# The sums' bank read by the Newton steps, weight pieces formed in a PSUM bank, and a dense list that knows what is left

## The chip, the cores and the metric

The kernel runs on one core of a Trainium2 chip, in one launch. The metric is the time of an execution in microseconds (us) on the device. Before the change the median of three runs is 644.42 us (642.54 to 644.81). The engines are named as the profile names them: PE (TensorE, matmuls), PEld (its weight loads), DVE (VectorE), ACT (ScalarE), POOL (GpSimd) and SP (SyncE, which issues the DMAs).

## The reference

Three layers follow each other. The attention works on 2 batches of 8 heads, 1152 keys, a head width of 64, and queries pooled by twos to 576:

```
q_pool = q.reshape(B, H, S // 2, 2, D).mean(axis=3)
scores = scale * q_pool @ k^T;  scores -= max over the keys
attn = exp(scores);  attn = attn / (sum over the keys + 1e-09)
out = attn @ v                            # 2 x 8 x 576 x 64
x = out.transpose(0, 2, 1, 3).reshape(1152, 512)
h = x @ w_in                              # 512 -> 2048
x = (max(h, 0) + log1p(exp(-|h|))) @ w_out         # -> 512
h = max(x @ w1, x @ w2, x @ w3)           # 512 -> 768, three times
out = h @ w_out2                          # -> 512
```

The dense weights arrive as 64-bit numbers, which the kernel reads as pairs of 32-bit words and turns into float32 itself.

## The kernel before

**Numbers in two halves.** A matmul of full float32 precision is made of three of the type fp32r: a value is cut into a high half (a copy to fp32r) and a low half (value minus high half), and high x high, low x high and high x low are added up in PSUM (`matmul3`, L1341).

**Attention.** The 16 heads are taken as 8 pairs. Each pair is prepared (load, pool the queries, transpose, cut into halves, send copies by DMA), then a first pass (`scores`, `part_max`, L977 on DVE) finds the maximum of each query's scores, and then units follow: two for each pair, three for the first, 17 in all, most of 288 queries. A unit goes through nine blocks of 128 keys and both heads: scores transposed (`st`, L1044 and L1045), their exponential (`p`, L1052 on ACT), a running sum over the blocks (`acc`, L1061, on POOL; in the last unit on DVE), and the product with the values (`x`, L1069). At a unit's end `sum_up` (L1081) adds over the keys by a matmul with ones into a PSUM bank `l`. `keep_sum` (L1086, ACT) copies it to SBUF as `rr` with 1e-9 added, `log_sum` and `near_inverse` (L1093, L1097, ACT) form exp(-ln(rr)) in `rz`, two Newton steps (`inverse`, L1103 and L1105, DVE) form -1/sum in `rr` out of `rr` and `rz`, both in SBUF, and `divide` (L1117, DVE) multiplies `x` from PSUM by it.

**Weight pieces.** The dense weights are cut into 56 pieces of 128 x 512. A piece is loaded (`raw`, SP), then `size_weight` (L232, ACT) and `bound_weight` (L237, POOL) treat its upper words, three integer steps on DVE (`float_weight`, L248, L257, L261) put the float32 number together in a tile `t`, `high_weight` (L276, ACT) and `low_weight` (L281, DVE) cut it. The first nine (NPRE) are formed while the attention runs, in a tile `t` in SBUF; the others in the dense part, where `t` lies in a PSUM bank, `b0`.

**Banks.** In the attention two of the eight PSUM banks hold `x`; the other six are a ring `s`, from which each block of scores, each transpose and each sum takes one and gives it back.

**Dense part.** The 1152 rows are three chunks of 384. `up` (h = x @ w_in, twelve matmuls for a block of 128 columns) is followed by the softplus (`size_h`, `lost1`, `lost2`, `log_h`, `lost3`, `soft`: ACT, DVE and POOL by turns), its halves (`high_g` ACT, `low_g` DVE), and, four blocks later, `down` (y). Gates (m) and `final` (o) follow.

**What sets the order.** All of it is issued in an order that a list planner (`Order.ordered`) writes. Each work item has an engine, a cost in us, a place (its priority), what it reads and writes, and perhaps a bank that it takes or frees. The planner moves a clock for each engine, takes the work that can begin first, and among those ready on its engine the one with the lowest place. The attention and the first pieces are one list, the dense part with the later pieces is a second one, whose engine clocks begin at 0. Each engine then works through its own queue in that order, so that a late item holds up what is behind it. The constants in AK, WINDOW and the costs in `order.add` only set this order.

Of the kernel before, what the change touches and what calls it, by code (L numbers as in the profile page):

```python
# [16 lines left out]
P = 128  # L17
# [16 lines left out]
AK = {"load": 30.79, "load1": -203.6, "q1": -64.7, "k1": -43.43, "v0": -70.5, "s0": -51.42, "v": -50.88, "q": -48.24, "k": -39.97, "pass": 7.12, "gap": 2.74, "values": 6.34, "sum": 8.99, "p1": -78.35, "p2": -9.81, "kl": 0.75}  # L34
WINDOW = 31.77
POOL_OF = {"tq": "s", "tk": "s", "tm": "s", "sum": "s"}
# [18 lines left out]
class Order:  # L55
# [6 lines left out]
    def __init__(self, **pools):  # L62
        self.work = []
        self.wrote = {}
        self.read = {}
        self.pools = pools
        self.got = {}

# [15 lines left out]
    def ordered(self):  # L84
# [6 lines left out]
        clear = dict.fromkeys(self.AFTER, 0.0)  # L91
# [7 lines left out]
        for _ in work:  # L99
# [26 lines left out]
            for m in users[n]:  # L126
                left[m] -= 1
                if not left[m]:
                    other = work[m][0]
                    ready[other][m] = max(  # L130
                        at[k] + (self.AFTER[work[k][0]] if work[k][0] != other or other in ("SP", "AQ") else 0.0)
                        for k in work[m][5]
                    )
        return [n for _, n in out]
# [3 lines left out]
def kernel(  # L138
# [100 lines left out]
    def float_weight(n, step):  # L239
        r, size = words[n][:2]  # L240
        if step == 0:
            if n < NPRE:
                words[n] += (conv.tile([P, C], I32, tag="t", bufs=2, name=f"t_{n}"),)
            else:
                words[n] += (pools["b"].tile([P, C], I32, tag="b0", name=f"t_{n}"),)
# [494 lines left out]
    else:  # L740
# [93 lines left out]
        def one(n):  # L834

            return tiles[n][:, 0] if n[0] == "t" else tiles[n]
# [253 lines left out]
        def log_sum(u):  # L1090
            tiles["rz", u] = sm.tile([P, HQ], F32, tag="rz", name=f"rz_{u}")
            W = UNIT[u][2]
            nc.scalar.activation(out=tiles["rz", u][:, :W], in_=tiles["rr", u][:, :W], func=AF.Ln)  # L1093

        def near_inverse(u):
            rz = tiles["rz", u][:, : UNIT[u][2]]
            nc.scalar.activation(out=rz, in_=rz, func=AF.Exp, scale=-1.0, accum_out=sums[:, 1, u : u + 1])  # L1097

        def inverse(u, step):
            W = UNIT[u][2]  # L1100
            rr, rz = tiles["rr", u][:, :W], tiles["rz", u][:, :W]
            if step == 0:
                nc.vector.tensor_tensor(out=rr, in0=rr, in1=rz, op=ALU.mult)  # L1103
            else:
                nc.vector.scalar_tensor_tensor(out=rr, in0=rr, scalar=2.0, in1=rz, op0=ALU.subtract, op1=ALU.mult)  # L1105

        def keep_values(u):
            W = UNIT[u][2]
            tiles["xc", u] = sm.tile([P, HQ], F32, tag=f"xc{u % 2}", name=f"xc_{u}")
            nc.scalar.copy(tiles["xc", u][:, :W], tiles["x", u][:, :W])  # L1110
            tiles["x", u] = tiles["xc", u]
# [28 lines left out]
        def name_of(n):  # L1140
            return f"b{n[0]}{n[1]}"

# [104 lines left out]
        def one_unit(u):  # L1247
# [7 lines left out]
            for j in range(NJ):  # L1255
# [7 lines left out]
                if j:  # L1263
                    engine = "DVE" if j in (ON_DVE[u % 2] if u + 1 < UNITS else LAST) else "POOL"
                    order.add(engine, 1.5 * part if engine == "POOL" else 1.25 * part, p, add_p, u, j, engine,
                              reads=[f"p{m % NPT}"] + ([f"p{(m - 1) % NPT}"] if j == 1 else []), writes=(f"acc{u % 2}",))
# [4 lines left out]
            if XB == 1:  # L1271
                order.add("ACT", 0.43, p, keep_values, u, reads=("x0",), writes=(f"xc{u % 2}",))
            n, p = next_bank("sum"), at + gap * NJ + AK["sum"] * part
            order.add("PE", 0.7 * part, p, sum_up, u, n, reads=(f"acc{u % 2}",), writes=(name_of(n),), take=n)
            order.add("ACT", 0.65, p - 3, keep_sum, u, n, reads=(name_of(n),), writes=(f"rr{u % 2}",), free=n)
            order.add("ACT", 0.42, p - 3, log_sum, u, reads=(f"rr{u % 2}",), writes=("rz",))
            order.add("ACT", 0.62, p - 3, near_inverse, u, writes=("rz",))
            order.add("DVE", 0.6, p - 3, inverse, u, 0, reads=("rz",), writes=(f"rr{u % 2}",))
            order.add("DVE", 0.6, p - 3, inverse, u, 1, reads=("rz",), writes=(f"rr{u % 2}",))
            order.add("DVE", 0.47 if XB == 2 else 0.6, p - 3, divide, u, reads=(f"rr{u % 2}", f"x{u % 2}" if XB == 2 else f"xc{u % 2}"), writes=(f"xy{u}",))  # L1280
# [20 lines left out]
        for n in range(NPRE + 3):  # L1301
            late = 1e6 + 10 * n
            order.add("SP", 0.6, late, load_weight, n, reads=k1_of(0, (2,)) if n < 3 else (), writes=(f"raw{n % 3}",))
            if n < NPRE + 2:
                order.add("ACT", 0.68, late + 1, size_weight, n, reads=(f"raw{n % 3}",), writes=(f"size{n % 2}",))
                order.add("POOL", 1.6, late + 1, bound_weight, n, writes=(f"size{n % 2}",))
            if n < NPRE:
                for step in range(3):
                    order.add("DVE", (1.2, 1.25, 1.25)[step], late + 2 + step, float_weight, n, step,
                              reads=(f"raw{n % 3}", f"size{n % 2}"), writes=(f"t{n % 2}",))  # L1310
                order.add("ACT", 0.61, late + 6, high_weight, n, reads=(f"t{n % 2}",), writes=(f"w{n}",))
                order.add("DVE", 1.05, late + 7, low_weight, n, reads=(f"t{n % 2}", f"w{n}"), writes=(f"wl{n}",))
# [40 lines left out]
    work = Order(b=NBANKS)  # L1353

# [318 lines left out]
```

## Time and profile before

| | |
|---|---|
| median of three runs | 644.42 us (642.54 to 644.81) |
| the profiled execution | 643.09 us |
| its span, first to last instruction | 641.3 us |
| mean granted clock of PE | 0.985 |
| busy: PE, DVE, ACT, POOL | 614.1, 445.8, 337.1, 410.1 us |
| DMA | 66.14 MB, mean 103 GB/s |

Busy time is the time in which an engine had an instruction under way; PE's matmuls are pipelined and their ends modelled, so that a busy PE isn't yet PE at its peak. The attention runs until about 272 us, the dense part from there on.

### The profile page before, as it was taken

To read this page: it belongs to the slowest core of one execution; us is meant where nothing else is said; L and a number is where in the kernel's file an instruction comes from. 1 tells how busy PE (TensorE), PEld (TensorE's weight loads), DVE (VectorE), ACT (ScalarE), POOL (GpSimd) and SP (SyncE) were. 2 spreads that over 40 slices of the span, in tenths; PEclk is the share of its full clock that TensorE was granted. 3 is DMA by queue.
4 is the path that set the end of the run, shared out by engine and by line. 5 is a ranking of instruction groups with operands and counts; after the bars stand their busy time and mean duration, and the time that the engine had idled before them with its cause. 6 is when DMAs were issued, how large, how long until landed. Compare 5 with 4: busy or idle time off the path is not lost.

```text
span 641.3 us, 10400 instructions
## 1 busy us (share of the span) xinstructions
PE 614.1 (96%) x3640; PEld 531.7 (83%) x3640; DVE 445.8 (70%) x779; ACT 337.1 (53%) x844; POOL 410.1 (64%) x338
## 2 busy tenths in 40 slices
PE   3999999999999999989999999999999999999995
PEld 2687776767676766678999999999999999999994
DVE  3946566899999997789889797886978731211221
ACT  4265566666565757576776766675754311112101
POOL 5287979999999999569977777887876200000000
PEclk9799999999999999989999999999999999999998
DMA  8785779768665721023333333421233201000001
GB/s 188 177 190 140 157 168 229 165 147 207 168 164 142 165 71 34 1 67 99 99 99 114 96 120 99 132 95 42 97 98 126 74 0 50 1 0 34 17 1 55
DMA packets 60574, 66.14 MB, mean 103 GB/s; under 512 B 22184, under 2 KB 48864, under 8 KB 60512
## 3 DMA queue, kind: packets, MB, share of 16 engines
q1 hardware_dynamic: 59664, 64.62, 38.2%
q10 hardware_dynamic: 848, 0.77, 0.5%
q8 instruction: 30, 0.49, 0.3%
q14 instruction: 32, 0.26, 0.1%
HBM read 43.52 MB, written 2.36 MB: 72 GB/s over the span
## 4 chain that ended last, share of the span: by engine, by line
PE 77%; DVE 14%; POOL 3%; ACT 2%; DMA 2%; issue 1%; SPq 1%; POOLq 0%; ACTq 0%; DVEq 0%
PE bank_h_m L1341 18%; PE bank_y L1341 15%; PE bank_h L1341 14%; PE x L1069 7%; PE bank_o L1341 6%; PE st L1044 5%; DVE nh L977 5%; PE s L966 4%; PE st L1045 3%; DVE rr L1105 2%; POOL acc L1061 2%; DVE t L248 2%; DVE t L261 1%; DVE t L257 1%; DMA k<-in_k_dram 1%
## 5 line engine op out<-in xcount | busy, mean ns | idle before, releaser
L1061 POOL TENSOR_TENSOR acc<-acc,p 128x576 f32<-128x576 f32 (+2 forms) x112 | 158.8, 1417 | 16.7 <-ACT p L1052 9.0
L1052 ACT ACTIVATE p<-st 128x288 f32<-128x288 f32 (+2 forms) x306 | 102.3, 399 | 67.5 <-PE st L1045 64.9
L977 DVE TENSOR_REDUCE nh<-s 128x1 f32<-128x384 f32 x216 | 105.9, 547 | 32.7 <-PE s L966 31.5
L1341 PE MATMUL bank_h_m<-x,wh 128*128 128x384 f32 x432 | 114.1, 338 | 0.0
L1341 PE MATMUL bank_h<-x,wh 128*128 128x384 f32 x384 | 106.0, 338 | 0.5 <-DVE gl L1418 0.5
L237 POOL TENSOR_SCALAR size<-size 128x512 f32<-128x512 f32 x56 | 87.3, 1559 | 17.3 <-ACT size L232 17.1
L1044 PE MATMUL st<-q,k 128*128 128x288 f32 (+2 forms) x306 | 90.7, 317 | 1.7 <-DVE nh L977 1.5
L1045 PE MATMUL st<-q,k 65*128 65x288 f32 (+2 forms) x306 | 83.4, 292 | 0.0
L1069 PE MATMUL x<-p,v 128*64 128x288 f32 (+2 forms) x612 | 80.8, 400 | 0.0
L1341 PEld LDWEIGHTS bank_h_m<-x,wh 128*128 128x128 f32 x432 | 78.8, 188 | 0.7
L1044 PEld LDWEIGHTS st<-q,k 128*128 128x128 f32 x306 | 57.9, 189 | 23.8 <-issue 11.0
L1341 PE MATMUL bank_h_m<-x,wl 128*128 128x384 f32 x216 | 72.9, 337 | 0.0
L1341 PEld LDWEIGHTS bank_h<-x,wh 128*128 128x128 f32 x384 | 70.3, 188 | 1.3 <-DVE gl L1418 0.8
L1341 PE MATMUL bank_y<-gh,wh 128*128 128x384 f32 x192 | 65.8, 343 | 3.7 <-ACT gh L1413 2.0
L1394 POOL TENSOR_TENSOR d<-e,d 128x384 f32<-128x384 f32 x48 | 48.9, 1020 | 29.7 <-DVE d L1387 28.3
L1341 PE MATMUL bank_y<-gl,wh 128*128 128x384 f32 x192 | 65.8, 342 | 0.0
L1341 PE MATMUL bank_y<-gh,wl 128*128 128x384 f32 x192 | 65.6, 342 | 0.0
L1341 PE MATMUL bank_h<-x,wl 128*128 128x384 f32 x192 | 64.8, 338 | 0.0
L1069 PEld LDWEIGHTS x<-p,v 128*64 128x64 f32 x612 | 39.2, 136 | 26.8 <-issue 7.7
L1045 PEld LDWEIGHTS st<-q,k 65*128 65x128 f32 x306 | 58.2, 190 | 0.0
L966 PE MATMUL s<-k,q 128*128 128x384 f32 x192 | 53.9, 381 | 2.5 <-DVE q L880 1.4
L1456 DVE TENSOR_TENSOR mg<-bank_h_m,mg 128x384 f32<-128x384 f32 x18 | 10.0, 555 | 61.3 <-PE bank_h_m L1341 61.3
(231 smaller groups left out, 1136.0 us busy)
## 6 DMA issues: line engine op xcount, KB each, us to landing
raw<-in_moe_w_out_dram SPq DMA_DIRECT2D x22, 512.0 KB, 3.6
raw<-in_moe_w_dram SPq DMA_DIRECT2D x18, 512.0 KB, 3.5
raw<-in_moe_w_in_dram SPq DMA_DIRECT2D x16, 512.0 KB, 6.3
k<-kh SPq DMA_DIRECT2D x28, 288.0 KB, 4.1
k<-in_k_dram SPq DMA_DIRECT2D x16, 288.0 KB, 5.6
v<-in_v_dram SPq DMA_DIRECT2D x16, 288.0 KB, 4.5
k<-kl SPq DMA_DIRECT2D x15, 288.0 KB, 6.9
q<-qh SPq DMA_DIRECT2D x29, 144.0 KB, 3.3
```

The costliest lines, as they stand in the source:

```text
L237: nc.gpsimd.tensor_scalar(out=size, in0=size, scalar1=SMALLEST, scalar2=None, op0=ALU.max)
L248: nc.vector.tensor_scalar(out=t, in0=size, scalar1=3, scalar2=REST, op0=ALU.logical_shift_left, op1=ALU.bitwise_and,)
L966: nc.tensor.matmul(o, q1[:, i, c0 : c0 + QB], k1[:, i, cols], start=True, stop=True)
L977: nc.vector.tensor_reduce(out=tiles["nh", pr][:, at, g : g + 1], in_=tiles[n][:, :BK], axis=AX.X, op=ALU.max, negate=True)
L1044: nc.tensor.matmul(to, k1[:, i, cols], q_of(pr, i, c0, c0 + W), start=True, stop=False)
L1045: nc.tensor.matmul(to, k3[:, i, cols], q3[:, i, c0 : c0 + W], start=False, stop=True)
L1052: nc.scalar.activation(out=tiles["p", u, j][:, some[0], :W], in_=tiles[n][:, :W], func=AF.Exp)
L1061: engine.tensor_tensor(out=acc, in0=first, in1=tiles["p", u, j][:, :, :W], op=ALU.add)
L1069: nc.tensor.matmul(x[halves(i), :W], tiles["v", pr][:, i, j], tiles["p", u, j][:, i, :W], start=(j == 0), stop=(j == NJ - 1),)
L1105: nc.vector.scalar_tensor_tensor(out=rr, in0=rr, scalar=2.0, in1=rz, op0=ALU.subtract, op1=ALU.mult)
L1341: nc.tensor.matmul(ps, lhs(a, kk), rhs(bb, kk), start=start and n == 0, stop=stop and n == last)
L1394: nc.gpsimd.tensor_tensor(out=d, in0=gs["e", i], in1=d, op=ALU.subtract)
```

## The change

Three things change, and constants of the planner with them.

The sum stays in its bank. `log_sum` and `near_inverse` now work in place in `rr`; the first Newton step reads the bank `l`, adds the 1e-9 and writes to the bank; the second reads the bank and writes `rr`. The bank is given back after the second step, not after `keep_sum`. The tile `rz` is gone.

The attention's nine pieces are formed in a bank of the ring `s`, taken before the first integer step and given back after the low half. The steps behind the first have place -100, ahead of nearly all other work.

The dense list begins with each engine's clock at what the attention's list has left for it beyond PE's end (`ahead`).

The costs of some items and the constants AK and WINDOW are new, and with them the order of the attention. `keep_values`, which wasn't used with two banks for `x`, is taken out.

```diff
-AK = {"load": 30.79, "load1": -203.6, "q1": -64.7, "k1": -43.43, "v0": -70.5, "s0": -51.42, "v": -50.88, "q": -48.24, "k": -39.97, "pass": 7.12, "gap": 2.74, "values": 6.34, "sum": 8.99, "p1": -78.35, "p2": -9.81, "kl": 0.75}
-WINDOW = 31.77
+AK = {"load": 40.43, "load1": -177.08, "q1": -125.74, "k1": -36.14, "v0": -104.52, "s0": -227.78, "v": -50.14, "q": -42.55, "k": -36.78, "pass": 5.13, "gap": 2.62, "values": 21.46, "sum": 8.86, "p1": -100.85, "p2": -11.22, "kl": 3.47}
+WINDOW = 28.28
...
-        clear = dict.fromkeys(self.AFTER, 0.0)
+        clear = {e: self.ahead.get(e, 0.0) for e in self.AFTER}
...
+        self.clear = clear
...
-        if step == 0:
+        if step == 0 and len(words[n]) == 2:
...
-            nc.scalar.activation(out=tiles["rz", u][:, :W], in_=tiles["rr", u][:, :W], func=AF.Ln)
+            nc.scalar.activation(out=tiles["rr", u][:, :W], in_=tiles["rr", u][:, :W], func=AF.Ln)
...
-            nc.scalar.activation(out=rz, in_=rz, func=AF.Exp, scale=-1.0, accum_out=sums[:, 1, u : u + 1])
+            nc.scalar.activation(out=rr, in_=rr, func=AF.Exp, scale=-1.0, accum_out=sums[:, 1, u : u + 1])
...
+            l, rr = one(n)[:, :W], tiles["rr", u][:, :W]
             if step == 0:
-                nc.vector.tensor_tensor(out=rr, in0=rr, in1=rz, op=ALU.mult)
+                nc.vector.scalar_tensor_tensor(out=l, in0=l, scalar=1e-9, in1=rr, op0=ALU.add, op1=ALU.mult)
             else:
-                nc.vector.scalar_tensor_tensor(out=rr, in0=rr, scalar=2.0, in1=rz, op0=ALU.subtract, op1=ALU.mult)
+                nc.vector.scalar_tensor_tensor(out=rr, in0=l, scalar=2.0, in1=rr, op0=ALU.subtract, op1=ALU.mult)
...
+        def early_float(n, step, b):
+            if step == 0:
+                words[n] += (bank(b, f"t_{n}").bitcast(I32),)
+            float_weight(n, step)
...
-            order.add("ACT", 0.65, p - 3, keep_sum, u, n, reads=(name_of(n),), writes=(f"rr{u % 2}",), free=n)
+            order.add("ACT", 0.68, p - 3, keep_sum, u, n, reads=(name_of(n),), writes=(r,))
+            order.add("ACT", 0.45, p - 3, log_sum, u, writes=(r,))
+            order.add("ACT", 0.64, p - 3, near_inverse, u, writes=(r,))
+            order.add("DVE", 0.47, p - 3, inverse, u, 0, n, reads=(r,), writes=(name_of(n),))
+            order.add("DVE", 0.47, p - 3, inverse, u, 1, n, reads=(name_of(n),), writes=(r,), free=n)
...
+                t = next_bank("w")
                 for step in range(3):
-                    order.add("DVE", (1.2, 1.25, 1.25)[step], late + 2 + step, float_weight, n, step,
-                              reads=(f"raw{n % 3}", f"size{n % 2}"), writes=(f"t{n % 2}",))
-                order.add("ACT", 0.61, late + 6, high_weight, n, reads=(f"t{n % 2}",), writes=(f"w{n}",))
-                order.add("DVE", 1.05, late + 7, low_weight, n, reads=(f"t{n % 2}", f"w{n}"), writes=(f"wl{n}",))
+                    order.add("DVE", 0.7, late + 2 if step == 0 else -100, early_float, n, step, t,
+                              reads=(f"raw{n % 3}", f"size{n % 2}"), writes=(name_of(t),), take=None if step else t)
+                order.add("ACT", 0.62, -100, high_weight, n, reads=(name_of(t),), writes=(f"w{n}",))
+                order.add("DVE", 0.7, -100, low_weight, n, reads=(name_of(t), f"w{n}"), writes=(f"wl{n}",), free=t)
...
+    if not exact:
+        work.ahead = {e: max(0.0, order.clear[e] - order.clear["PE"]) for e in ("ACT", "DVE", "POOL")}
```

Of the new costs not shown, POOL's additions go from 1.5 to 1.53 (the first of a unit 1.62) and `bound_weight` from 1.6 to 1.75.

## Rows read from the trace of the kernel before

**Rows 1.** the chain of waits, dense part: start us, us, engine, tile, line, instructions.
```profile
471.52 4.24 PE bank_y L1341 x24
```

**Rows 2.** busy time by stretch; the first row names the columns.
```profile
core 0: us, PE busy (x) PEld busy (x) DVE busy (x) ACT busy (x) POOL busy (x), PEclk, DMA share, GB/s
0.00:40.00 40.00, 29.47 (x163) 21.17 (x164) 22.51 (x52) 15.59 (x46) 18.36 (x33) 0.87 0.84 197
...
64.00:117.00 53.00, 52.48 (x354) 38.22 (x353) 32.97 (x67) 31.70 (x95) 45.48 (x36) 1.00 0.75 179
117.00:264.00 147.00, 142.73 (x932) 101.00 (x933) 140.09 (x211) 95.83 (x277) 142.53 (x94) 1.00 0.55 134
...
272.00:302.00 30.00, 25.76 (x135) 24.02 (x135) 25.44 (x45) 22.45 (x50) 24.52 (x23) 0.94 0.26 79
```

**Rows 3.** the chain of waits, 176 to 236 us.
```profile
190.01 1.80 DVE t L261
...
198.76 0.46 DVE xy L1117
```

**Rows 4.** groups by line, VectorE, 117 to 264 us: xcount, busy us, mean ns.
```profile
L261 DVE SCALAR_TENSOR_TENSOR t<-raw,t 128x512 int32<-128x512 int32 x9 | 14.8, 1643 | 0.3
L1105 DVE SCALAR_TENSOR_TENSOR rr<-rr,rz 128x288 f32<-128x288 f32 x10 | 14.0, 1397 | 0.3
L257 DVE SCALAR_TENSOR_TENSOR t<-raw,t 128x512 int32<-128x512 int32 x9 | 13.1, 1453 | 0.1
L248 DVE TENSOR_SCALAR t<-size 128x512 int32<-128x512 int32 x9 | 11.7, 1296 | 0.0
L281 DVE TENSOR_TENSOR wl<-t,wh 128x512 fp32r<-128x512 f32 x9 | 9.5, 1056 | 0.0
L1103 DVE TENSOR_TENSOR rr<-rr,rz 128x288 f32<-128x288 f32 x10 | 7.6, 761 | 3.5 <-ACT rz L1097 3.5
```

**Rows 5.** groups by line, VectorE, 302 to 520 us.
```profile
L281 DVE TENSOR_TENSOR wl<-t,wh 128x512 fp32r<-128x512 f32 x43 | 29.7, 690 | 12.0 <-ACT wh L276 11.5
L257 DVE SCALAR_TENSOR_TENSOR t<-raw,t 128x512 int32<-128x512 int32 x42 | 29.1, 693 | 1.1
L248 DVE TENSOR_SCALAR t<-size 128x512 int32<-128x512 int32 x42 | 29.1, 692 | 2.7
```

**Rows 6.** the tile t, 117 to 264 us: ns min/median/max, first and last start.
```profile
L248 DVE TENSOR_SCALAR t<-size x9: 417/1470/1639, 123.7 to 241.3; 128x512 int32<-128x512 int32 x9
```

**Rows 7.** groups by line, POOL, 64 to 117 us.
```profile
L1061 POOL TENSOR_TENSOR acc<-acc,p 128x576 f32<-128x576 f32 x24 | 34.1, 1419 | 5.7 <-ACT p L1052 3.6 <-ACT mr L1004 0.7
```

**Rows 8.** groups by line, POOL, 117 to 264 us.
```profile
L1061 POOL TENSOR_TENSOR acc<-acc,p 128x576 f32<-128x576 f32 x68 | 105.0, 1544 | 4.8 <-ACT mr L1004 0.3
L237 POOL TENSOR_SCALAR size<-size 128x512 f32<-128x512 f32 x11 | 19.7, 1790 | 0.0
```

**Rows 9.** groups by line, POOL, 302 to 520 us.
```profile
L237 POOL TENSOR_SCALAR size<-size 128x512 f32<-128x512 f32 x41 | 61.4, 1499 | 17.3 <-ACT size L232 17.1
```

**Rows 10.** order of time, PE: start us, us, instruction [idle before <-releaser].
```profile
263.88 0.71 PE L1081 MATMUL l<-acc,ones 128*64 128x288 f32 x4 [1.24 <-POOL acc L1061]
...
271.75 0.44 PE L1341 MATMUL bank_h<-x,wh 128*128 128x384 f32 x1
...
284.49 0.51 PE L1341 MATMUL bank_y<-gh,wh 128*128 128x384 f32 x1 [2.03 <-ACT gh L1413]
...
289.64 0.44 PE L1341 MATMUL bank_y<-gh,wh 128*128 128x384 f32 x1 [1.72 <-DVE gl L1418]
```

**Rows 11.** order of time, ScalarE, the same stretch.
```profile
278.63 0.59 ACT L276 CAST wh<-t 128x512 fp32r<-128x512 f32 x1 [3.06 <-DVE t L261]
279.11 0.50 ACT L1381 ACTIVATE e<-bank_h 128x384 f32<-128x384 f32 x1
```

**Rows 12.** order of time, POOL, the same stretch.
```profile
273.99 4.18 POOL L290 TENSOR_TENSOR x<-xy,x 128x384 fp32r<-128x384 f32 x4 [8.21 <-ACT x L287]
```

**Rows 13.** waits, 117 to 264 us: us in total, times, longest us.
```profile
PEld st L1044 <- DVE nh L977: 4.3, 10, 1.3
```

More of the change, by code (lines that the diff above doesn't have):

```diff
@@ L67, in __init__ @@
         self.got = {}
+        self.ahead = {}
     def add(self, engine, cost, place, f, *args, reads=(), writes=(), take=None, free=None):
@@ L1264, in one_unit @@
                     engine = "DVE" if j in (ON_DVE[u % 2] if u + 1 < UNITS else LAST) else "POOL"
-                    order.add(engine, 1.5 * part if engine == "POOL" else 1.25 * part, p, add_p, u, j, engine,
+                    order.add(engine, (1.53 if j > 1 else 1.62) * part if engine == "POOL" else 1.25 * part, p, add_p, u, j, engine,
                               reads=[f"p{m % NPT}"] + ([f"p{(m - 1) % NPT}"] if j == 1 else []), writes=(f"acc{u % 2}",))
@@ L1270, in one_unit @@
                           reads=[f"p{(u * NJ + j) % NPT}" for j in js] + [f"v{y}"], writes=(f"x{u % XB}",))
-            if XB == 1:
-                order.add("ACT", 0.43, p, keep_values, u, reads=("x0",), writes=(f"xc{u % 2}",))
             n, p = next_bank("sum"), at + gap * NJ + AK["sum"] * part
             order.add("PE", 0.7 * part, p, sum_up, u, n, reads=(f"acc{u % 2}",), writes=(name_of(n),), take=n)
-            order.add("ACT", 0.65, p - 3, keep_sum, u, n, reads=(name_of(n),), writes=(f"rr{u % 2}",), free=n)
[L1276 to L1280, printed above, removed]
+            r, x = f"rr{u % 2}", f"x{u % XB}"
+            order.add("ACT", 0.68, p - 3, keep_sum, u, n, reads=(name_of(n),), writes=(r,))
[3 more added lines that the diff above has]
+            order.add("DVE", 0.47, p - 3, inverse, u, 1, n, reads=(name_of(n),), writes=(r,), free=n)
+            order.add("DVE", 0.47, p - 3, divide, u, reads=(r, x), writes=(f"xy{u}",))
             if (u + 1 == UNITS or UNIT[u + 1][0] != pr) and pr < NC:
@@ L1305 @@
                 order.add("ACT", 0.68, late + 1, size_weight, n, reads=(f"raw{n % 3}",), writes=(f"size{n % 2}",))
-                order.add("POOL", 1.6, late + 1, bound_weight, n, writes=(f"size{n % 2}",))
+                order.add("POOL", 1.75, late + 1, bound_weight, n, writes=(f"size{n % 2}",))
             if n < NPRE:
+                t = next_bank("w")
                 for step in range(3):
-                    order.add("DVE", (1.2, 1.25, 1.25)[step], late + 2 + step, float_weight, n, step,
-                              reads=(f"raw{n % 3}", f"size{n % 2}"), writes=(f"t{n % 2}",))
-                order.add("ACT", 0.61, late + 6, high_weight, n, reads=(f"t{n % 2}",), writes=(f"w{n}",))
-                order.add("DVE", 1.05, late + 7, low_weight, n, reads=(f"t{n % 2}", f"w{n}"), writes=(f"wl{n}",))
+                    order.add("DVE", 0.7, late + 2 if step == 0 else -100, early_float, n, step, t,
+                              reads=(f"raw{n % 3}", f"size{n % 2}"), writes=(name_of(t),), take=None if step else t)
+                order.add("ACT", 0.62, -100, high_weight, n, reads=(name_of(t),), writes=(f"w{n}",))
+                order.add("DVE", 0.7, -100, low_weight, n, reads=(name_of(t), f"w{n}"), writes=(f"wl{n}",), free=t)
         for n in order.ordered():
```

13 lines of the change are left out of this document (3 added, 10 removed).

## Prediction

> **What bounds the kernel now.** I read the table of stretches first, because the share of busy time over the whole span (PE 96%) hides that the stages have different limits. From 302 us on PE has no gap of note: 24 matmuls take 4.24 us there, 0.177 us each [rows 1], and the change alters no matmul. What can be won lies before. In the first 40 us PE is busy for 29.5; from 64 to 117 us for 52.5 of 53; from 117 to 264 us for 142.7 of 147; from 272 to 302 us for 25.8 of 30 [rows 2].
>
> Busy shares flatter PE, because the ends of its matmuls are modelled, so I count issues instead. From 64 to 117 us PE starts 354 matmuls in 53 us, 0.150 us each; from 117 to 264 us 932 in 147 us, 0.158 us each [rows 2]. The mix is much the same (scores, values, maxima passes), so the second stretch runs 5% slower than the same work did before it. What is different in it is VectorE: 33 of 53 us busy in the early stretch, 140.1 of 147 in the later one, where the attention's weight pieces have begun; POOL is at 142.5 of 147 as well [rows 2].
>
> The chain of waits, read next, agrees: from 187 to 230 us it hardly leaves VectorE. Its longest pieces are steps of t (the integer work that forms a weight piece, 1.80 us) and steps of rr (the Newton steps); a step of the same size with one input in PSUM, xy, takes 0.46 us [rows 3]. The groups by line, read third, say what these cost: with t and the sums in SBUF a step of t takes 1.30 to 1.64 us on average, a Newton step 0.76 or 1.40 us [rows 4]. The same t in a PSUM bank, as the dense part has it, takes 0.69 us for each step, for the low half too [rows 5].
>
> **The change, part by part.** I sum against the profiled execution: 643.09 us, of which 641.3 are the span and 1.8 lie around it. The median of the three runs, 644.42, is 1.3 us above that.
>
> *Newton steps on the sums' bank.* Ten units fall into 117 to 264 us. Their L1105 and L1103 take 14.0 + 7.6 = 21.6 us [rows 4]; at the 0.46 us of xy [rows 3], the row with the same operands (PSUM and SBUF in, 288 columns), 20 x 0.46 = 9.2. VectorE is spared 12.4 us. No row has such a step that also writes PSUM; the bounds are 0.46 and the present 0.76, and I take 0.46.
>
> *Weight pieces in a bank.* Nine pieces, five steps each, four on VectorE: 14.8 + 13.1 + 11.7 + 9.5 = 49.1 us [rows 4]; at 0.69 us [rows 5] 36 steps are 24.8. Spared: 24.3 us. The first step is not slow by nature: its fastest run in this stretch took 0.417 us [rows 6], so in a bank it can cost 0.28 us more than it could at best. The Trainium skill, in "VectorE: DVE Perf Modes", section "Why PSUM operands drop a tier", says why: an fp32 instruction with an operand in PSUM loses the mode that does two elements in a cycle. By that rule alone the nine first steps would lose 2.5 us on VectorE; by the mean of their rows (1.30 against 0.69) they gain 5.5.
>
> Together VectorE goes from 140.1 to 140.1 - 36.7 = 103 us of work in this stretch: it stops being the bound. What is late next? POOL and PE.
>
> POOL: its additions take 1.42 us in the early stretch [rows 7] and 1.54 in the later, its bound on a piece 1.79 [rows 8] against 1.50 in the dense part [rows 9]. It slows down where the slow VectorE steps are. If these go, 68 x 0.125 + 11 x 0.29 = 11.7 us of POOL's 142.5 go too: 131. The Trainium skill has this as a rule ("SBUF — State Buffer", section "Who interferes with whom"): a VectorE instruction with two inputs in SBUF and a GpSimd instruction that reads SBUF exclude each other for the whole instruction, and one with at most one input in SBUF doesn't take part. The 0.46 beside the 1.40 and the 1.42 beside the 1.54 us agree.
>
> PE: at the early stretch's 0.150 us the 932 matmuls take 139.5 us instead of 147, 7.5 less. So after the change PE needs 139.5, POOL 131, VectorE 103 of whatever the stretch becomes. PE becomes the bound, with POOL 6% behind, and two nearly full engines that feed each other don't pack perfectly. I take 5.5 us. The bounds: 1 (the one plain wait that surely shrinks, 1.24 us of PE for POOL's last sum [rows 10]) and 7.5.
>
> *The dense list's beginning.* The planner took the engines as free when PE begins the dense part, at 271.75 us [rows 10]. In fact ACT and VectorE still have the last unit's sum, inverse and division to do. So ACT's queue was written with the high half of a new piece ahead of the first chunk's softplus, and ACT stood 3.06 us for VectorE's t, until 278.63; only then, at 279.11, it took up the first h, whose twelve matmuls, begun at 271.75, need 2.1 [rows 11]. POOL spent 273.99 to 278.17 on four pieces of x needed much later [rows 12]. PE paid at 284.49 (2.03 us waiting for gh) and 289.64 (1.72 for gl), and its granted clock averages 0.94 in this stretch, so a part of it ran at 1.2 instead of 2.4 GHz [rows 2, 10]. From 272 to 302 us 135 matmuls start [rows 2]; at 0.177 us [rows 1] these are 23.9 us, so 6 of the 30 are lost. Told of the leftover work, the planner puts the first h ahead of the piece, and the gates on VectorE ahead of the next pieces. VectorE is busy for 25.4 of these 30 us [rows 2], so a shorter stretch has little room on it, and I take 4.5. Bounds: -1.5 (another order that only moves the wait) and 6.
>
> *Banks.* The ring of score banks has six. Each piece now holds one for its five steps (4 x 0.69 + 0.62 = 3.4 us, by the rows and the new planned cost for ACT), each sum for some 2 us longer (0.45 + 0.64 + 0.47 + 0.47 planned). That is a wait that the change adds: queued behind it on PE are the next scores. PE's loads of scores wait ten times for a bank that a maximum returns in this stretch now, 4.3 us in all, 0.43 at a time [rows 13], in good part because VectorE is late. Between nothing and the second rival's price I take 1 us lost.
>
> *Order and places.* New constants shift priorities: values later within a unit, pair 1's queries earlier, send_q3, send_k3 and v of pair 0 earlier in SP's queue, and pieces that have begun go first. No DMA is added or taken away; their engines are 0.75 busy in the early stretch and 0.55 in the later [rows 2], so that a transfer moved ahead of pair 1's loads has room. In the early stretch PE has 0.5 us of idle time to win; in the first 40 us it has 10.5 [rows 2], but that stretch begins with transfers from memory that have to land before any matmul, and whose number and size stay. I take 0, with 1.5 us to either side. The planner's other new costs move nothing but order.
>
> Sum: -5.5 - 4.5 + 1 + 0 = -9, 634.1 us by the profiled execution and 635.4 by the median. Forecast: 634.5.
>
> **Rivals.** *PE was the bound all along.* For it: 142.7 of 147 us busy, and only 4.3 us of visible gaps. Then VectorE's relief is hidden and only the seam pays, with the 1.24 us at the end: 643.1 - 4.5 - 1.2 = 637.4. Against it: 0.158 against 0.150 us per matmul, and the chain on VectorE.
>
> *The seam only moves.* VectorE, 85% busy in 272 to 302 us, can't deliver earlier whatever the order: attention's 5.5 less 1 lost remain, 638.6. For it: that share. Against it: ACT stood idle for 3.06 us at the decisive place.
>
> *Everything packs.* PE 7.5, the seam 6, no bank missed, and 1.5 from the beginning: 628.1. For it: POOL and VectorE both get slack. Against it: PE never did better than 0.150.
>
> *Too few banks (slower).* Place: PE's score bursts from 117 to 264 us and around every sum. Price: 26 holds (9 pieces, 17 sums), two misses each, of 0.43 us [rows 13]: 22 us, so 643.1 - 10 + 22 = 655. It is slower by over 0.5% from 31 misses on, 1.2 for each hold. For it: bursts of six scores use the whole ring. Against it: so far few waits are for banks, and a piece that has begun is finished first.
>
> **How the numbers follow.** A measurement of this kernel can't tell less than 0.5% (3.2 us) from no change. Forecast (630 to 637): 0.53. PE bound all along: 0.15, of which a fifth would end within 0.5%. Seam only moves: 0.12, a quarter within 0.5%. Everything packs: 0.1. Too few banks: 0.1, half within 0.5%, half slower. Sums: faster 0.84, same 0.11, slower 0.05. The range reaches from everything packed at 627 to 641, where the two mild rivals have room.
>
> **What would show it.** Right: L1105 and L1103 near 0.46 us and t near 0.69 throughout; VectorE near 105 us for the work of today's 117 to 264; POOL's additions at 1.42 to 1.45; the chain of waits on PE or POOL there; no wait of PE over 1 us after the first dense matmul, and the granted clock full. Wrong: PE's loads waiting for ACT's exponentials or for t's and the sums' banks by more than 10 us in all; the dense part's first down projection waiting again. If PE's pace stays 0.158 us with VectorE at 70%, the bound was misread.

## The result, and the profile after

The changed kernel takes 629.62 us (median of four runs, 628.77 to 630.23), the kernel before on the same chip 644.11 (642.54 to 644.81): 0.978 of it, 95% interval 0.976 to 0.980. The gain is 14.5 us; 9 were forecast, and the time lies inside the range of 627 to 641.

To see where it came from, I cut each span at two marks: the start of the attention's first sum on PE and that of its last (the 17th).

| us | to the first sum | first to last sum | last sum to end | span |
|---|---|---|---|---|
| before | 40.7 | 230.4 | 370.2 | 641.3 |
| after | 40.8 | 219.5 | 366.7 | 627.0 |
| difference | +0.1 | -10.9 | -3.5 | -14.3 |

So three quarters of the gain lie in the attention and a quarter at the beginning of the dense part. The experiments below are compared by the same marks. In the profiled executions of four of them (without the leftover work, Newton steps in SBUF, VectorE's steps twice, POOL's bound twice) PE ran mostly at the lower of its two clock levels from 32 to 40 us (granted clock 0.52 to 0.55, 43 to 45 matmuls against 78) and reached the first sum some 5 us later, which their times contain and the stretches between the marks don't.

Where single pairs of heads are compared, a pair's time runs from the last sum of the pair before it to its own last sum.

Busy time by stretch, after (columns as in [rows 2]):

```profile
40.00:64.00 24.00, 24.00 (x191) 19.23 (x188) 15.10 (x35) 14.41 (x51) 18.46 (x18) 1.00 0.68 156
64.00:117.00 53.00, 53.00 (x359) 38.79 (x359) 33.62 (x72) 32.53 (x98) 46.15 (x36) 1.00 0.71 177
117.00:255.00 138.00, 137.96 (x926) 99.90 (x925) 102.39 (x203) 91.04 (x273) 125.79 (x92) 1.00 0.56 137
...
264.00:290.00 26.00, 24.27 (x138) 23.65 (x136) 22.16 (x42) 20.79 (x45) 24.41 (x23) 1.00 0.29 96
```

The same stretches of the kernel before; the last row lies, as the one above does, from 3 to 29 us behind PE's first dense matmul:

```profile
40.00:64.00 24.00, 23.93 (x180) 18.73 (x179) 16.37 (x37) 14.41 (x50) 18.10 (x17) 1.00 0.60 135
...
117.00:255.00 138.00, 134.97 (x877) 95.46 (x877) 132.08 (x205) 89.68 (x260) 133.92 (x88) 1.00 0.59 142
...
274.80:300.80 26.00, 21.76 (x113) 20.02 (x112) 23.27 (x42) 18.51 (x40) 22.51 (x22) 0.93 0.27 82
```

From 117 to 255 us PE now has 926 matmuls under way instead of 877, one every 0.149 us, and is all but never idle. The trace's shapes give the same in columns (the width of what each matmul moves): 269,568 instead of 255,744, 5.4% more. VectorE is down from 132 to 102 us and POOL from 134 to 126, with eight weight pieces in the stretch where there were nine. Already from 40 to 64 us there are 11 more matmuls than before, but narrower ones are among them: in columns it is 43,872 against 42,528, 3% more.

VectorE's groups by line from 117 to 255 us, after (xcount, busy us, mean ns, then idle time before), answer to [rows 4]:

```profile
L259 DVE SCALAR_TENSOR_TENSOR t<-raw,t 128x512 int32<-128x512 int32 x8 | 5.6, 697 | 0.3
L263 DVE SCALAR_TENSOR_TENSOR t<-raw,t 128x512 int32<-128x512 int32 x8 | 5.6, 696 | 0.3
L283 DVE TENSOR_TENSOR wl<-t,wh 128x512 fp32r<-128x512 f32 x8 | 5.5, 686 | 2.6 <-ACT wh L278 2.6
L250 DVE TENSOR_SCALAR t<-size 128x512 int32<-128x512 int32 x8 | 5.5, 685 | 0.0
...
L1106 DVE SCALAR_TENSOR_TENSOR rr<-l,rr 128x288 f32<-128x288 f32 x10 | 4.6, 457 | 0.3
...
L1104 DVE SCALAR_TENSOR_TENSOR l<-l,rr 128x288 f32<-128x288 f32 x10 | 4.6, 456 | 3.2 <-ACT rr L1098 3.2
```

And POOL's, answering to [rows 8]:

```profile
L1063 POOL TENSOR_TENSOR acc<-acc,p 128x576 f32<-128x576 f32 x67 | 95.2, 1421 | 10.8 <-ACT p L1054 6.9
L239 POOL TENSOR_SCALAR size<-size 128x512 f32<-128x512 f32 x10 | 15.8, 1584 | 0.0
```

The chain of waits from 117 to 264 us, summed by line, first before and then after (where the dense part begins at 260.9 us):

```profile
by line: DVE nh L977 17.0%; PE x L1069 12.0%; POOL acc L1061 7.6%; PE st L1044 7.2%; DVE t L248 6.3%; DVE rr L1105 5.9%; PE s L966 5.5%; PE st L1045 5.1%; DVE t L261 4.9%; DVE t L257 4.2%; DMA k<-kh 3.1%; DVE rr L1103 2.4%; DVE wl L281 2.4%
```

```profile
by line: PE x L1071 30.6%; PE st L1046 18.3%; PE st L1047 15.2%; PE s L968 14.3%; DVE acc L1063 4.3%; PE l L1083 3.9%; PE tk L922 2.0%; issue 1.5%; PE s L965 1.4%; PE s L964 1.4%; ACT p L1054 1.1%; PE tm L1001 1.0%; PE tq L849 0.9%; DVE t L
```

VectorE's maxima, piece and Newton steps, 43% of the chain before, have given way to PE's own matmuls. Where PE's loads wait for a maximum's bank, [rows 13] has barely moved: 4.4 us in ten waits, shorter at the longest:

```profile
PEld st L1046 <- DVE nh L979: 4.4, 10, 0.4
```

At the dense part's start (PE, ScalarE and VectorE in order of time, after; start us, us, instruction, idle before):

```profile
260.93 0.44 PE L1341 MATMUL bank_h<-x,wh 128*128 128x384 f32 x1
...
275.55 0.45 PE L1341 MATMUL bank_y<-gh,wh 128*128 128x384 f32 x1 [1.73 <-DVE gl L1420]
...
290.60 0.45 PE L1341 MATMUL bank_h<-x,wh 128*128 128x384 f32 x1 [0.57 <-DVE gl L1420]
```

```profile
262.25 0.59 ACT L278 CAST wh<-t 128x512 fp32r<-128x512 f32 x1
...
263.73 0.48 ACT L1383 ACTIVATE e<-bank_h 128x384 f32<-128x384 f32 x1
```

```profile
272.43 0.56 DVE L1408 SCALAR_TENSOR_TENSOR bank_h<-bank_h,d 128x384 f32<-128x384 f32 x1
272.89 0.68 DVE L250 TENSOR_SCALAR t<-size 128x512 int32<-128x512 int32 x1
273.61 0.69 DVE L259 SCALAR_TENSOR_TENSOR t<-raw,t 128x512 int32<-128x512 int32 x1
274.34 0.70 DVE L263 SCALAR_TENSOR_TENSOR t<-raw,t 128x512 int32<-128x512 int32 x1
274.94 0.55 DVE L1420 TENSOR_TENSOR gl<-bank_h,gh 128x384 fp32r<-128x384 f32 x1
```

ScalarE takes up the first h 2.8 us after PE's first dense matmul, where it took 7.4 [rows 10, 11]. PE's two stops of 2.03 and 1.72 us [rows 10] have become one of 1.73, and the granted clock no longer falls (1.00 against 0.93 in the two last rows above). The stop that is left has its cause in VectorE's queue: three steps of a later weight piece (2.05 us) stand between the softplus' last step and the low half gl that PE wants.

### The profile page after: what moved, and what is told of

Its sections match the earlier page's. It is cut to its first block, busy times and chain, and to the rows that moved or that the text cites. A ratio compares the mean times of both kernels' runs of the same rounds, so it can differ in the third digit from the quotient of the medians.

```text
span 627.0 us, 10422 instructions
## 1 busy us (share of the span) xinstructions
PE 606.7 (97%) x3640; PEld 530.5 (85%) x3640; DVE 408.9 (65%) x779; ACT 333.6 (53%) x844; POOL 396.1 (63%) x338
## 4 chain that ended last, share of the span: by engine, by line
PE 91%; DVE 4%; ACT 1%; DMA 1%; issue 1%; POOL 1%; SPq 0%; DVEq 0%; ACTq 0%; POOLq 0%
PE bank_h_m L1341 18%; PE bank_h L1341 15%; PE bank_y L1341 15%; PE x L1071 11%; PE st L1046 7%; PE s L968 6%; PE bank_o L1341 6%; PE st L1047 6%; PE l L1083 1%; PE tk L922 1%; DVE acc L1063 1%; DMA k<-in_k_dram 1%; PE s L964 1%; PE s L965 1%; DVE nh L979 1%
## 5 line engine op out<-in xcount | busy, mean ns | idle before, releaser
L1063 POOL TENSOR_TENSOR acc<-acc,p 128x576 f32<-128x576 f32 (+2 forms) x112 | 150.3, 1342 | 21.2 <-ACT p L1054 14.6
L979 DVE TENSOR_REDUCE nh<-s 128x1 f32<-128x384 f32 x216 | 107.2, 550 | 52.1 <-PE s L968 45.6
L1054 ACT ACTIVATE p<-st 128x288 f32<-128x288 f32 (+2 forms) x306 | 100.8, 399 | 68.2 <-PE st L1047 66.4
L239 POOL TENSOR_SCALAR size<-size 128x512 f32<-128x512 f32 x56 | 84.8, 1517 | 24.4 <-ACT size L234 24.3
L1046 PE MATMUL st<-q,k 128*128 128x288 f32 (+2 forms) x306 | 88.7, 311 | 0.0
L1405 POOL TENSOR_TENSOR d<-u,d 128x384 f32<-128x384 f32 x48 | 48.9, 1020 | 3.5
```

Source lines behind the costliest of these rows:

```text
L239: nc.gpsimd.tensor_scalar(out=size, in0=size, scalar1=SMALLEST, scalar2=None, op0=ALU.max)
L979: nc.vector.tensor_reduce(out=tiles["nh", pr][:, at, g : g + 1], in_=tiles[n][:, :BK], axis=AX.X, op=ALU.max, negate=True)
L1046: nc.tensor.matmul(to, k1[:, i, cols], q_of(pr, i, c0, c0 + W), start=True, stop=False)
L1054: nc.scalar.activation(out=tiles["p", u, j][:, some[0], :W], in_=tiles[n][:, :W], func=AF.Exp)
L1063: engine.tensor_tensor(out=acc, in0=first, in1=tiles["p", u, j][:, :, :W], op=ALU.add)
L1405: nc.gpsimd.tensor_tensor(out=d, in0=gs["u", i], in1=d, op=ALU.add)
```

## The experiments

### The dense list's beginning, taken out and put in alone

Taken out of the kernel after:

```diff
-    if not exact:
-        work.ahead = {e: max(0.0, order.clear[e] - order.clear["PE"]) for e in ("ACT", "DVE", "POOL")}
```

> The changed kernel without the line that starts the dense list with what is left over. The attention is the same, instruction for instruction, until PE's last sum at 260 us. Theory (the list's start keeps ScalarE from standing behind a piece): the dense start loses 3 to 4.5 us again, with a wait of PE of 2 us for gh, 632.5 to 634 us. Rival (the shorter VectorE steps alone made the dense start shorter): 629 to 631 us.

Measured: 634.33 us (632.83 to 637.05), 0.984 of before (0.979 to 0.989). First to last sum 219.5, as after; last sum to end 370.2, as before. PE's stops come back, 1.34 us for gh and 2.83 for gl.

The same lines put into the kernel before, with nothing else of the change:

> The kernel before with the one line that starts the dense list with what is left over, and nothing else; its attention stays as it was. Theory (the list's start is worth what e2 lost, 4 to 5 us): 639 to 640.5 us, against 644 before. Rival (VectorE, 85% busy at the dense start, can't deliver earlier whatever the order): 642.5 us or more.

Measured: 640.33 us against 644.3, 0.994 of it (0.990 to 0.997). First to last sum 230.45, as before; last sum to end 367.0. One stop of PE is left, 2.33 us for gl.

What follows: this part is worth 3.2 to 3.6 us with either attention, and nothing between the first and the last sum. The first theory's 3 to 4.5 us hold, the second's 4 to 5 are a little too many; both rivals are out.

### Operands and constants, apart

Constants of before in the kernel after:

```diff
-AK = {"load": 40.43, ...}
-WINDOW = 28.28
+AK = {"load": 30.79, ...}
+WINDOW = 31.77
```

> The changed kernel with AK and WINDOW of the kernel before; the costs of the items, the PSUM operands and the dense list's start stay as changed. Theory (operands and the list's start did it; VectorE no longer binds from 117 us on): only the 2.5 us gained ahead of 117 us can be the constants' doing, so 629.6 to 632.5 us. Rival (the new constants bought the order that packs PE): half of the attention's 10.7 us goes, 635 us or more.

Measured: 637.27 us (636.99 to 638.04), 0.989 of before (0.985 to 0.994). First to last sum 229.7: of the 10.9 us only 0.7 are left, as the rival has it; last sum to end is 364.9. The new costs of the items and the place of the begun pieces stay in this run; they weren't taken out by themselves.

The other way round, the same two lines of after in the kernel before and nothing else (its costs and places stay):

> The kernel before with the new AK and WINDOW and nothing else; operands in SBUF, planned costs of before. Theory (constants and operands only work together, as e1 and e3 have it): VectorE's steps are as long as before, so the constants alone gain no more than the 1.5 us ahead of 64 us, 642 to 645 us. Rival (the constants carry the attention's gain by themselves): 636.5 us, the 7.6 us that e1 lost.

Measured: 641.72 us (641.09 to 646.79), 0.996 of before (0.993 to 0.999). First to last sum 228.4, 2.0 less than before.

Neither half gives much; together they give 10.9. In the run with the old constants the shorter steps did pay at first: the third, fourth and fifth pairs took 29.6, 30.3 and 29.5 us against 30.6, 31.6 and 31.6 before. Then the seventh took 31.7 against 27.2. ScalarE and PE there, in order of time:

```profile
228.18 0.66 ACT L234 ACTIVATE size<-raw 128x512 f32<-128x512 f32 x1 [3.67 <-DMA raw<-in_moe_w_out_dram]
```

```profile
229.20 1.05 PE L968 MATMUL s<-k,q 128*128 128x384 f32 x3 [3.02 <-ACT p L1054]
```

ScalarE stood 3.67 us for a weight piece's raw words, with the exponentials that PE needed behind it in its queue. The load had been issued at 222.1 us and took 6 us to land; the planner counts 0.6 for a load and 2.6 for its landing. So I gave that run an honest price:

```diff
-            order.add("SP", 0.6, late, load_weight, n, ...
+            order.add("SP", 3.6, late, load_weight, n, ...
```

> e1 (the change with the old AK and WINDOW) with one planned cost more: a load of a piece is planned at 3.6 instead of 0.6 us, so with 2.6 us to land at 6.2, near the 6.0 us that it took in e1. Theory (with the old constants VectorE's shorter steps do pay, but five pieces are bunched between 203 and 223 us and ScalarE's queue stands 3.7 us for a load that the plan has landed early): the stretch from the first to the last sum, 229.7 us in e1 and 219.5 with the new constants, falls to 223 to 226 us, the time to 631 to 634 us. Rival (the old constants' order of scores, values and pieces is what costs): 228 us or more from first to last sum, 636 us or more.

Measured: 632.53 us (632.36 to 632.87), 0.981 of before (0.977 to 0.985). First to last sum 224.6, the seventh pair 25.7, no wait of ScalarE for a load there. The other pairs are within 0.7 us of the run without the price, so the 5.2 us gained between the marks lie where the wait was.

As a control the same price in the kernel after, whose trace has no such wait:

> The kernel after, with a weight piece's load planned at 3.6 us instead of 0.6 (6.2 with its landing, as the trace of the old-constants run measured it). Theory: that cost paid with the old constants only because there ScalarE's weight step really stood 3.7 us for a load in 206 to 230 us; the kernel after has no such wait in the attention, so here nothing is left to win: first to last sum 219.5 within 1.5 us, the time 628.5 to 631. Rival A: an honest load cost is worth a few us whatever the constants (loads spread, pieces never bunched): first to last sum 214 to 217, the time 624 to 627. Rival B: the constants of the kernel after fit their own wrong cost, and any change of a planned cost loses part of what they gave: first to last sum 222 to 227, the time 632 to 637.

Measured: 629.11 us (628.69 to 630.33), 0.976 of before (0.972 to 0.979). First to last sum 219.6: nothing changes, as the theory has it; where no such wait stands, the price is worth nothing.

What follows: with the shorter steps, the order is worth 10.2 us (229.7 to 219.5), of which 5.2 are one late load. The other 5 belong to constants whose single effects I haven't separated.

The sixth sum parts the attention (it starts at 117.5 us before and 115.2 after; the first weight piece's steps begin behind it, at 123.7 [rows 6] and 121.3):

| us | first to sixth sum | sixth to last sum |
|---|---|---|
| before | 76.8 | 153.6 |
| constants of after alone | 74.9 | 153.5 |
| constants of before in the kernel after | 75.5 | 154.3 |
| the same, with the honest price | 75.5 | 149.1 |
| after | 74.4 | 145.1 |

Ahead of the pieces either half alone brings a good part of the 2.4 us. Behind, where VectorE was full, the constants alone bring 0.1 us, the shorter steps with the old constants 4.5 once that load is planned right, and both together 8.5.

### The pieces' bank: where it saves

The pieces' integer steps in SBUF again, in the order of after (the bank is still held):

```diff
-                words[n] += (bank(b, f"t_{n}").bitcast(I32),)
+                bank(b, f"t_{n}")
```

> The changed kernel with its order kept, but t of the nine pieces in SBUF instead of a PSUM bank (the bank is reserved and unused). Theory (VectorE's time and POOL's slowed additions): t takes 1.3 to 1.7 us a step again, VectorE gets 24 us and POOL some 7 us more work in the attention, PE's pace falls from 0.149 to 0.154 us a matmul, 634 to 638 us. Rival (order did it): within 1 us of 629.6.

Measured: 657.22 us (656.72 to 661.27), 1.022 of before (1.016 to 1.028): slower than the kernel before, and far from both the theory (634 to 638) and the rival. First to last sum 248.0, 28.5 more than after, all of it behind the sixth sum. Yet VectorE isn't full (the stretch 117 to 255 us, then 3.5 us out of it):

```profile
117.00:255.00 138.00, 124.58 (x771) 87.04 (x766) 105.64 (x181) 74.04 (x219) 107.67 (x76) 0.94 0.54 132
```

```profile
127.50:131.00 3.50, 3.50 (x17) 1.83 (x17) 1.16 (x3) 0.64 (x3) 2.45 (x2) 0.64 0.46 110
```

ScalarE and PE ahead of it, in order of time:

```profile
125.92 0.62 ACT L278 CAST wh<-t 128x512 fp32r<-128x512 f32 x1 [3.79 <-DVE t L263]
126.44 0.25 ACT L1006 CAST mr<-tm 3x128 fp32r<-3x128 f32 x1
```

```profile
126.75 1.01 PE L968 MATMUL s<-k,q 128*128 128x384 f32 x2 [2.53 <-ACT mr L1006]
127.69 2.80 PE L1071 MATMUL x<-p,v 128*64 128x288 f32 x12
```

The three integer steps run 1.22, 1.63 and 1.62 us on average where the order was written for 0.7. (The kernel before had such steps too, in an order written for 1.2, and took 230.4.) ScalarE's high half waits 3.79 us for the last of them; behind it stands the small cast mr that the next scores need; PE stops for 2.53 us and then runs twelve matmuls in 2.80 us instead of the 1.68 that twelve such took at 121.36 us, at a granted clock of 0.64 over that stretch. Over the 138 us both count: 771 matmuls at 0.149 us are 115 us; of the other 23 PE is idle for 13.4, and some 10, by this estimate, go to the lower clock (0.94 on average). ScalarE's waits for a piece's last integer step sum up, from 117 to 255 us (us in total, times, longest), to

```profile
ACT wh L278 <- DVE t L263: 19.4, 6, 3.8
```

against 4.1 in five after.

That could still be VectorE and POOL excluding each other rather than the mere length of the steps. So I kept every operand in PSUM and did each VectorE step of a piece twice (and the division three times), which gives the length without the shared operands:

```diff
+            words[n] = kept
+            float_weight(n, step)
...
+        def early_low(n):
+            low_weight(n)
+            low_weight(n)
...
+            for _ in range(3):
                 nc.vector.scalar_tensor_tensor(out=xy[:, c, t0 : t0 + W], ...
```

> The changed kernel, operands in PSUM, order kept; each of VectorE's four steps of the nine early pieces is issued twice in place, and each unit's division three times (the results are the same). VectorE gets 24.8 + 15.6 us of work, what the change took from it, none of it with two SBUF inputs. Theory A (the time of VectorE's steps is what costs, since ScalarE's and PE's queues stand behind them): most of e3's loss comes back, 648 us or more. Theory B (the loss in e3 is POOL and VectorE shutting each other out): within 4 us of 629.6, VectorE having 35 us free.

Measured: 664.08 us (662.02 to 666.52), 1.028 of before. First to last sum 248.7, within 0.7 of the run with SBUF steps. VectorE, POOL and the rest from 117 to 255 us, POOL's additions, and the largest waits that matter:

```profile
117.00:255.00 138.00, 126.86 (x781) 89.70 (x780) 113.69 (x224) 76.00 (x223) 105.06 (x77) 0.94 0.56 135
```

```profile
L1063 POOL TENSOR_TENSOR acc<-acc,p 128x576 f32<-128x576 f32 x56 | 79.2, 1414 | 27.2 <-ACT p L1054 24.5
```

```profile
ACT wh L278 <- DVE t L263: 17.1, 6, 3.1
...
PE s L968 <- ACT mr L1006: 5.2, 3, 1.7
```

POOL's additions run at their full speed (1.414 us), VectorE is at 114 of 138, and the same wait of ScalarE is nearly as long, 17.1 us: the three integer steps ahead of it last 4.2 us here and 4.5 in SBUF. So long steps in the queues are enough for a loss of this size, without shared operands: theory A holds, theory B doesn't. That they are the whole of the other run's loss isn't shown: this run gives VectorE some 40 us more work, that one by its rows some 22, and the pairs don't lose alike (the third 2.4 us here and 4.3 there, the seventh 10.1 and 8.4). A run with the pieces' steps alone made longer, the divisions left as they are, would tell; it wasn't made.

### The Newton steps alone

Both steps in SBUF again with their tile rz, the order and the held bank as after:

```diff
-                nc.vector.scalar_tensor_tensor(out=l, in0=l, scalar=1e-9, in1=rr, op0=ALU.add, op1=ALU.mult)
+                nc.vector.tensor_tensor(out=rr, in0=rr, in1=rz, op=ALU.mult)
...
-                nc.vector.scalar_tensor_tensor(out=rr, in0=l, scalar=2.0, in1=rr, op0=ALU.subtract, op1=ALU.mult)
+                nc.vector.scalar_tensor_tensor(out=rr, in0=rr, scalar=2.0, in1=rz, op0=ALU.subtract, op1=ALU.mult)
```

> The changed kernel with its order kept, but the Newton steps on rr and rz in SBUF as before. Theory: 17 pairs of steps take 2.1 us instead of 0.9 again, 20 us more for VectorE over the attention and some 4 us for POOL, 631.5 to 634 us, and the 2.5 us ahead of 117 us are lost here, where no piece is formed. Rival (two steps each 15 us are too few to matter while VectorE has a quarter of its time free): within 1 us of 629.6.

Measured: 632.94 us (630.38 to 635.33), 0.982 of before (0.976 to 0.987). First to last sum 221.0, 1.4 more than after, 1.0 of it before the third sum; of the 3.3 us between the times only this, by the marks, is the steps' own. The time lies in the theory's range, but not for its reason: a pair of steps takes 1.44 us, not 2.1. Its Newton steps, 117 to 255 us:

```profile
L1107 DVE SCALAR_TENSOR_TENSOR rr<-rr,rz 128x288 f32<-128x288 f32 x10 | 9.3, 929 | 0.3
L1105 DVE TENSOR_TENSOR rr<-rr,rz 128x288 f32<-128x288 f32 x10 | 5.1, 513 | 3.2 <-ACT rz L1099 3.2
```

They are slower than in the bank (0.457), but far from the 1.397 and 0.761 us of [rows 4]. Why they are shorter here, with the pieces out of SBUF, wasn't tried.

### POOL and the banks

`bound_weight` twice for the eleven early pieces, 16 us more for POOL:

```diff
+        def bound_twice(n):
+            bound_weight(n)
+            bound_weight(n)
...
-                order.add("POOL", 1.75, late + 1, bound_weight, n, writes=(f"size{n % 2}",))
+                order.add("POOL", 1.75, late + 1, bound_twice, n, writes=(f"size{n % 2}",))
```

> The changed kernel with POOL's bound issued twice for each of the eleven early pieces (same result): 16.4 us more for POOL, 10 of them from 117 to 255 us, which takes it from 126 to about 141 of 138. Theory (POOL is the next bound, close behind PE): 5 to 9 us slower, 635 to 638. Rival (POOL has slack where it counts, being ahead of PE by a unit): under 2 us slower.

Measured: 636.53 us (634.34 to 639.91), 0.987 of before (0.982 to 0.991). First to last sum 224.6, 5.0 more than after, as the theory has it, nearly all of it in the last two pairs. In the stretch, POOL is at 132 of 138:

```profile
117.00:255.00 138.00, 135.45 (x893) 97.25 (x890) 101.52 (x206) 87.71 (x262) 132.15 (x97) 0.99 0.57 140
```

A ring of five banks instead of six:

```diff
-        order = Order(t=int(ONE), s=8 - XB - 3 * ONE)
+        order = Order(t=int(ONE), s=7 - XB - 3 * ONE)
```

> The changed kernel with a ring of five score banks instead of six, planned anew. Theory (banks are no longer scarce, since VectorE returns them in time; the pieces' and sums' holds cost nothing): up to 3 us slower, 630 to 633 us. Rival (the holds of pieces and sums live on the sixth bank): PE waits once for a bank in each of the 17 sums and 9 pieces, 0.43 us each, and in bursts of scores, 640 us or more.

Measured: 646.29 us (644.36 to 649.3), 1.003 of before (1.0007 to 1.0047). First to last sum 236.2, 16.7 more than after; the third and fourth pairs take 35.6 and 34.4 us instead of 29.4. The rival's size came, but not its bursts of waits: no single wait of PE holds this time (from 104 to 174 us the longest, a weight load's, is 0.8 us), and between the two sums PE is idle for 3.9 us in all. The list, short of a bank, puts the work in another order. Among what comes late are the raw loads, whose issue on SP waits for a piece's steps (the same stretch; us in total, times, longest):

```profile
SPq L224 <- DVE t L263: 11.5, 3, 5.5
```

So six banks suffice and five don't; how the lost time divides between the new order and the missing bank stays open.

### Eight early pieces

In the kernel after the ninth piece is formed across the seam (its steps run from 260.1 to 263.6 us). One piece less in the attention's list:

```diff
-NPRE = 9
+NPRE = 8
```

> The changed kernel with eight pieces (NPRE = 8) formed in the attention instead of nine; the ninth, which came at 260 us between the last unit's additions and its Newton steps, goes to the dense list. Theory (that piece holds a bank and 3 us of VectorE just where the dense part starts: waits of PE of 0.30, 1.73 and 0.57 us): the stretch from the last sum to the end falls from 366.7 to 364.9 us, which e1 had with no such piece, 627 to 628.5 us. Rival (the dense list has then a piece more in its first 25 us, VectorE being 85% busy there): 629.5 to 632 us.

Measured: 629.23 us (628.93 to 629.27), 0.976 of before (0.972 to 0.980): no difference from after. Last sum to end is 367.3 us, not the 364.9 of the theory: PE's wait moves from 275.6 us (1.73 for gl) to 286.8 (1.32 for wl). Why the run with the old constants has 364.9 stays open. Neither this run nor the one with honest loads beats the kernel after by more than a measurement can tell.

## Why the prediction was right, and where its terms were off

| term | forecast | measured |
|---|---|---|
| attention, 117 us to the last sum | -5.5 | -8.4 |
| banks | +1 | 0 |
| before 117 us (forecast as order and places) | 0 | -2.5 |
| dense list's beginning | -4.5 | -3.5 |
| sum | -9 | -14.4 |

The attention's 10.9 us divide so: from 117 to 255 us PE has 49 more matmuls, at 0.149 us 7.3 us; by 117 us its rows are 714 - 697 = 17 matmuls ahead, 2.5 us (2.4 by the sixth sum); 1.1 are left for the stretch to the last sum, where PE's 1.24 us for POOL's last addition [rows 10] is gone.

**Right.** The prices of the steps: 0.685 to 0.697 us for the pieces' (0.69 forecast), 0.457 for Newton's (0.46), 1.421 for POOL's additions (1.42); only the bound on a piece stayed above its 1.50, at 1.584. VectorE's work: 102.4 us, with the ninth piece's four steps 105, against 103 in the sum. PE as the next bound, at the early stretch's pace: from the first to the last sum it is busy for 219.47 of 219.51 us. POOL close behind, which the run with POOL's bound twice confirms: 16 us more on it cost 5. The seam doesn't merely move, and PE wasn't the bound all along.

The Trainium skill's rule cited in the prediction ("SBUF — State Buffer", section "Who interferes with whom") agrees with the rows again, as POOL's 1.54 us fell to 1.42 when VectorE's second SBUF operand went. The prediction left out a limit of it: a VectorE instruction with one input in SBUF stays out of the conflict only outside the modes that use both of VectorE's ports. The first integer step, with its one input, took 0.417 us at best and 1.30 on average [rows 4, 6], which agrees with the limit. But the run with VectorE's steps twice costs as much with that conflict gone: here the rule explains the length of a step, not by itself the time. The Trainium skill's other rule ("VectorE: DVE Perf Modes", "Why PSUM operands drop a tier") agrees too: the first integer step never ran below 0.68 us in the bank, where 0.417 was its best in SBUF [rows 6]. The section speaks of fp32, and the step's numbers are int32. Its mean still fell from 1.30 to 0.685.

**The steps that were mis-sized.** The time lies in the range, but just below the 630 to 637 us that were thought likeliest. "two nearly full engines that feed each other don't pack perfectly. I take 5.5 us": they do pack, PE is busy 137.96 of 138 us, nearly all of the upper bound of 7.5 came by 255 us, and with the 1.1 behind it, which the prediction named as its lower bound and didn't add, the 8.4 lie outside the bounds. "I take 0, with 1.5 us to either side" for order and places missed 2.5 us before 117 us. The prediction looked for idle time of PE in the early stretch and found 0.5 us; but PE's columns grow in all of the stretches up to there (by 1,088, 1,344 and 1,888 in 0 to 40, 40 to 64 and 64 to 117 us, 2.2 us at the later stretch's 1.95 columns a nanosecond), also where its row reads as full (23.9 of 24 us). Nor is this the order's doing alone: ahead of the sixth sum the constants by themselves bring 1.9 of the 2.4 us, the shorter steps with the old constants 1.3, and with the Newton steps back in SBUF 1.0 are lost. And the order's share isn't an addend at all: the operands without the new constants give 0.7 us (5.8 with one load's price put right), the constants without the operands 2.0, both 10.9. Argued from VectorE's sum alone, the forecast holds only where the order written beforehand fits the new durations; the prediction didn't ask that of its 5.5.

The bank term was 0 (waits of PE's loads for a maximum's bank 4.3 us before, 4.4 after, and PE itself never idle), so the slower rival didn't come; but the ring is used up, as five banks show. The beginning of the dense part gave 3.5, not 4.5. A stop of 1.73 us is left there, behind a piece's three steps, but whether it is the missing 1 us isn't shown: with eight pieces that stop went and another came. My sign "no wait of PE over 1 us" failed there; the one on the granted clock held, and the first down projection, at 272.07 us, doesn't wait.

Of the rivals "everything packs" (628.1) ended nearer to the 629.6 us than the forecast did: its attention was nearly right (7.5 where 8.4 came, no bank missed, 1.5 from the beginning where 2.5 came), its 6 us at the seam were not.

## What to carry to other kernels

In an order written beforehand, ask of each step how long it really takes against its plan and whose queue stands behind it, not only how busy its engine is: with VectorE at 77% busy, pieces' steps up to 2.3 times as long as planned cost 28 us, and one load planned at 3.2 us that took 6 cost 5, while Newton steps twice as long as planned (0.929 against 0.47 us) cost 1.4. So when operations change their length, rewrite the costs and the order with them, and price the two together rather than one after the other. Where PE is called full, count its matmuls, or better their columns, per us: from the first to the last sum PE was busy for 225.3 of 230.4 us before, and yet nearly the same columns (427,648, then 426,752) came to fit into 219.5. More than half of what was won lay inside the busy time.

## What the runs showed of the hardware

A stop of PE costs more than its length: after the 2.53 us in the run with SBUF steps, the twelve matmuls that followed took 2.80 us instead of 1.68, and the granted clock was 0.64 from 127.5 to 131 us, so most of that stretch ran at 1.2 instead of 2.4 GHz; over 117 to 255 us it averages 0.94 there and 1.00 after. Not every stop does it: behind the 1.73 us at the dense part's start after the change, it stayed at 1.00.

Loads of equal size took 3.5 to 7.1 us to land. From 60 to 262 us of the kernel after (table of issues: xcount, KB each, median us to landing):

```profile
raw<-in_moe_w_in_dram SPq DMA_DIRECT2D x8, 512.0 KB, 7.1
raw<-in_moe_w_out_dram SPq DMA_DIRECT2D x3, 512.0 KB, 3.6
```

The difference can't be put down to the matrix. The trace has the landing of three of these loads only: the 7.1 is one load, the second of three of w_in issued within 1 us (at 96.8, 97.2 and 97.8 us), and the 3.6 stands for two of w_out, each issued with no other such load near it. The load of w_out that cost 5 us in the run with the old constants took 6; one of w_in had been issued half a microsecond behind it. Whether company in the queues or the matrix makes a load slow wasn't tried.
